# Attention: value products on every second query tile, the next head's hash products in front of them, exponentials placed by tile

## The chip, the cores and the metric

The kernel runs on one core of a Trainium2 chip. The metric is the device time of one execution in microseconds, the median of several runs. A core has engines with a queue each, which run side by side and wait for each other through semaphores: TensorE (PE in the profile, its weight loads PEld), VectorE (DVE), ScalarE (ACT), GpSimd (POOL), and SyncE (SP), whose queue here issues transfers alone.

## What is computed

Three stages, each fed by the one before. The change lies in the first.

```python
q_bits = (einsum('bhsd,dk->bhsk', q, proj) > 0)     # 6 hash bits
k_bits = (einsum('bhsd,dk->bhsk', k, proj) > 0)
mask = q_bucket[:, :, :, None] == k_bucket[:, :, None, :]
scores = where(mask, q @ k.T / sqrt(64), -1e9)
attn = softmax(scores);  x = attn @ v               # 2 x 8 heads, 768 x 64
x = moe(x)     # 1536 tokens of 512, top 1 of 8 experts, 512 -> 1024 -> 512
out = (x @ w_a) * (x @ w_b) @ w_out
```

## The kernel before

Attention goes through 16 heads (h) one after the other. A head has six query tiles (t) of 128 queries, and a tile is one step g = 6h + t of a single loop. The order of work on each engine is the order in which this loop writes it; nothing is moved afterwards. A step does the following.

- `scores(g + 1)` (L158, L159): four products on TensorE that put the next tile's 128 x 768 scores, hash bits included, into PSUM (`s`, two buffers).
- `smax(g + 1)` on VectorE: a minimum over the scores (L164, `mm`) and one small SCALAR_TENSOR_TENSOR (L165) that makes the scale and bias `sb` of the exponential.
- Work of other heads on TensorE, the "fill": the value products `av_step` of the head before (L200, `AV_AT` says which of its six key tiles go to which query tile), the output products `o_out` of two heads before (L238, tile 4), the hash products `hash_mm` of the next head (L128, `m`).
- `tposes(g, 0)` and `tposes(g, 1)` (L185, `tp`, two buffers of one half tile each): six transposes of the tile's exponentials `p`. Each half is copied from PSUM to `pt` ("eviction"), by ScalarE (L189) or VectorE (L191), as table `ev` says.
- `sexp(g + 1)` on ScalarE (L172, `p`): the next tile's exponentials. The table `se` gives for each t where it is written: 0 before the evictions of tile g, 1 between them, 2 behind them.
- Preparation of head h + 2: `split_a` on ScalarE (L103) writes `tq` at tile 2 and `tk` at tile 4 (`sa`: behind position 2 of tile 2, at position 1 of tile 4); `split_b` makes the rests, `bq` on VectorE and GpSimd (L115, L116) and `bk` on GpSimd alone (a TENSOR_TENSOR, L118, and a CAST, L119).
- At tile 1 `hash_codes` (L142) turns the hash products into bits, and four transfers on the SP queue (L147) put them into `tq` and `tk` of the next head. `load(h + 3)` is also written at tile 1, ahead of all else; its buffer is the one that the hash products of head h + 1 read last.
- At tile 5 `o_evac` on VectorE copies the finished value products out of PSUM (L220).

ScalarE, VectorE and GpSimd take their instructions strictly in the written order, which these lines of the step fix:

```python
side(0)          # sexp if se[t] == 0, hash_codes at tile 1
tposes(g, 0)
side(1)          # sexp if se[t] == 1, then split_a at tile 4
tposes(g, 1)
side(2)          # sexp if se[t] == 2, split_a at tile 2, split_b
```

The first head (h = 0) and the last (h = 15) have other fill; the expert layer (from about 268 us) and the last layer follow, and neither is touched.

Of the kernel before, what the change touches and what calls it, by code (L numbers as in the profile page):

```python
# [21 lines left out]
N, DM, E, FF, F2 = 1536, 512, 8, 1024, 1536  # L22
C = 224
GR = ((0, 6), (6, 4), (10, 2))
K = {'se': (0, 1, 2, 1, 1, 2), 'ev': (0, 0, 0, 1, 0, 1, 0, 0, 0, 1, 0, 0), 'avl': (), 'oul': 0, 'hml': 0, 'hc': ((0, 0), (0, 2), (1, 1), (2, 1)), 'sa': ((2, 2), (4, 1)), 'sb': ((3, 2), (4, 2)), 'ext': (1, 0, 2, 4, 7, 8), 'hm0': 0, 'hc0': ((1, 0), (1, 2), (3, 0), (4, 1))}
C_ID, C_TRI, C_THR, C_REV, C_TOK, C_IOTA, C_BASE, C_SLOT = 0, 128, 256, 258, 266, 278, 279, 287
CW = C_SLOT + C
FAR = 1024.0
AV_AT = {1: (0, 1), 2: (2,), 3: (3, 4), 5: (5,)}


@with_exitstack
def attn_moe_kernel(ctx: ExitStack, tc: tile.TileContext, xin, cst, projd, wblk, wmoe, w2in, out):
# [29 lines left out]
    pos = const.tile([128, 12], F32, name="pos")  # L63
# [29 lines left out]
    def load(h, first=()):  # L93
        X[h] = xp.tile([128, 2 * S], F32, tag="x", name="x")
        for i in range(2):
            after(nc.sync.dma_start(out=X[h][:, i * S:(i + 1) * S], in_=xin[h, :, i * S:(i + 1) * S]), first)
        V[h] = vp.tile([128, NT, D], F32, tag="v", name="v")
        nc.sync.dma_start(out=V[h], in_=xin[h, :, 2 * S:].rearrange("p (k d) -> p k d", d=D))
# [24 lines left out]
    def hash_mm(h, order=range(4)):  # L123
        p = (ps_m if h or 2 in order else ps_a).tile([128, 512], F32, tag="m" if h or 2 in order else "a", name="m")
        for j in order:
            i = j // 2
            hp_[h, j] = p
            PE.matmul(  # L128
                p[32 * j:32 * j + 32, :384], pst[:, 32 * i:32 * i + 32], X[h][:, j * 384:(j + 1) * 384],
                start=True, stop=True, skip_group_check=True,  # L130
            )
# [19 lines left out]
    def scores(g):  # L151
        h, t = divmod(g, NT)
        p = ps_s.tile([128, 2, 512], F32, tag="s", name="s")
        st[g] = p
        qs = slice(t * 128, t * 128 + 128)
        for c in range(2):
            sl = slice(c * 384, c * 384 + 384)
            PE.matmul(p[:, c, :384], T[h, 0][:76, qs], T[h, 1][:76, sl], start=True, stop=False)  # L158
            PE.matmul(p[:, c, :384], B[h, 0][:, qs], B[h, 1][:, sl], start=False, stop=True)  # L159

    def smax(g):
        m = mm[:, g % 4]
        sb = sm.tile([128, 2], F32, tag="sb", name="sb")
        DVE.tensor_reduce(out=m[:, 1:2], in_=st[g][:, :, :384], axis=AX.XY, op=ALU.min)  # L164
        DVE.scalar_tensor_tensor(  # L165
            out=sb, in0=m[:, 1:2].to_broadcast([128, 2]), scalar=BIG / 2, in1=m, op0=ALU.is_le, op1=ALU.mult
        )
        scl[g], nbs[g] = sb[:, 0:1], sb[:, 1:2]
# [9 lines left out]
    def tposes(g, half):  # L178
# [8 lines left out]
        src = ps[:, :384].rearrange("p (a b) -> p a b", a=3)  # L187
        if K["ev"][2 * t + half] == 0:
            ACT.activation(o, src, ACTF.Copy)  # L189
# [5 lines left out]
    def av_step(h, k):  # L195
        if k == 0:
            av[h] = ps_a.tile([128, 512], F32, tag="a", name="av")
        v = V[h][:, k]
        for c in range(2):
            PE.matmul(  # L200
                av[h][c * 64:(c + 1) * 64, :384], v, PT[h][:, k, c * 384:(c + 1) * 384],
                start=(k == 0), stop=(k == NT - 1), skip_group_check=True,
            )
# [261 lines left out]
    def w_load(n, part):  # L465
        if n < 64:
            RAW[n, part] = wraw.tile([128, 512], F32, tag=f"wr{part}", name=f"wr{part}")
            nc.sync.dma_start(out=RAW[n, part], in_=wmoe[n // 8, n % 8, :, part * 512:(part + 1) * 512])
# [126 lines left out]
    with tc.manual_schedule():  # L595
# [49 lines left out]
        def set_up(k):  # L645
            if k == 0:
                split_b(1, 0)
                POOL.tensor_copy(held, pt_[0][:, 0:1])
            elif k == 1:
                split_b(1, 1)  # L650
            elif k == 2:
                POOL.memset(oh, 0.0)
                zero = wraw.tile([128, 512], F32, tag="wr0", name="zero")
                POOL.memset(zero, 0.0)
                zeros.append(zero)
                DVE.tensor_copy(tri, cs[:, C_TRI:C_TRI + 128])
            elif k == 5:
                DVE.tensor_scalar(
                    out=tokc.bitcast(I32)[:, :, 0], in0=cs[:, C_TOK:C_TOK + 12], scalar1=-float(E * C), scalar2=None,
                    op0=ALU.add,  # L660
                )
                DVE.tensor_scalar(
                    out=base2, in0=cs[:, C_BASE:C_BASE + 8], scalar1=1.0 / 128, scalar2=None, op0=ALU.mult
                )
# [3 lines left out]
        L = NHD - 1  # L668
        acts = (x0_load, lambda: x_split(0), lambda: (w_split(0, 0, POOL), w_split(0, 1, POOL)), lambda: x_split(1), lambda: x_split(2),
                lambda: w_split(1, 0, POOL))  # L670
        extra = {}
        for at, f in zip(K["ext"], acts):
            extra.setdefault(divmod(at, NT), []).append(f)
        NG = NHD * NT
        qa, qb = (0, 4), (4, 2)
        for g in range(NG):
            h, t = divmod(g, NT)
            if t == 1 and h + 3 < NHD:
                load(h + 3)
            if g + 1 < NG:  # L680
                scores(g + 1)
                smax(g + 1)
            if g < NT:
                set_up(g)
            if 2 * NT <= g < 2 * NT + (E * C + N) // 256:
                for i in (g - 2 * NT,):
                    nc.sync.dma_start(
                        out=xr[i * 256:(i + 1) * 256].rearrange("(p r) d -> p r d", p=128),
                        in_=zeros[0].unsqueeze(1).to_broadcast([128, 2, 512]),
                    )  # L690
            if g == 6 * NT:
                for n in range(4):
                    for part in range(2):
                        w_load(n, part)
            if g == 10 * NT + 1:
                r = router(0)
                todo = [r["s1"], r["s1b"], None, lambda: (r["s2"](), r["s2c"]()), r["s2b"], r["s4"], r["s4b"]]
                for f in r["sc"]:
                    todo += [f, None]
                todo += [r["s4c"], r["s3"], r["s5"]]  # L700
            early, late = [], []
            if h < L:
                if h:
                    for k in AV_AT.get(t, ()):
                        early.append(lambda k=k: av_step(h - 1, k))
                if h > 1 and t == 4:
                    (late if K["oul"] else early).append(lambda: o_out(h - 2))
                if t == (0 if h else K["hm0"]):
                    (late if K["hml"] else early).append(lambda: hash_mm(h + 1))
            elif t < 3:  # L710
                av_step(h - 1, 2 * t)
                av_step(h - 1, 2 * t + 1)
                if t == 0:
                    o_out(h - 2)
                if t == 2:
                    o_evac(h - 1)
            elif t == 3:
                o_out(h - 1)
            else:
                k = 3 * (t - 4)  # L720
                av_group(h, qa, (k, k + 1, k + 2))
                if t == 5:
                    o_evac(h, qa)
            for f in early:
                f()
            if h and h < L and t == 5 and not K["avl"].count(5):
                o_evac(h - 1)
            if g > 10 * NT + 1 and todo:
                f = todo.pop(0)
                if f:  # L730
                    f()

            def side(pos):
                if g + 1 < NG and K["se"][t] == pos:
                    sexp(g + 1)
                for i in range(2):
                    if h + 2 < NHD and K["sa"][i] == (t, pos):
                        split_a(h + 2, i)
                    if h + 2 < NHD and K["sb"][i] == (t, pos):
                        split_b(h + 2, i)  # L740
                if h < L and (t, pos) == (1, 0):
                    hash_codes(h + 1)

            side(0)
            tposes(g, 0)
            side(1)
            tposes(g, 1)
            for f in late:
                f()
            if h and h < L and t == 5 and K["avl"].count(5):  # L750
                o_evac(h - 1)
            side(2)
            for f in extra.get((h - L + 1, t), ()):
                f()
# [578 lines left out]
```

## Time and profile before

| | |
|---|---|
| median of 3 runs | 750.09 us (749.51 to 750.5) |
| the profiled execution, its own time | 749.55 us |
| its span, first to last instruction | 747.7 us |
| TensorE busy | 728.7 us (97% of the span) |
| VectorE, ScalarE, GpSimd busy | 527.3, 434.4, 279.4 us |
| granted TensorE clock, mean | 0.997 |

The time of a run is about 1.9 us more than the span; what lies around the span is not in the trace. Busy time of TensorE is modelled from starts and sizes, so a busy TensorE may still be waiting a little. Rows of the timeline give the start of an instruction (or of several alike in a row, "x6") and its length; two starts tell how long a piece of work really took, the wait included. A wait in square brackets is idle time of the engine just before, and who ended it.

### The profile page before, as it was taken

How to read it: one execution, taken by the hardware profiler on the slowest of the kernel's cores; microseconds unless marked ns; L12 is line 12 of the kernel's file. 1: busy time of each engine (PE TensorE's matmuls, PEld its weight loads, DVE VectorE, ACT ScalarE, POOL GpSimd, SP SyncE). 2: the span in 40 equal slices, each digit the busy share in tenths (PEclk: the TensorE clock that was granted, in tenths of full speed). 3: DMA queues.
4: the chain of work that ended last, by engine and by line, in shares of the span. 5: the costliest groups of instructions: out<-in, count | busy, mean ns of one | idle time of the engine just before them, and what ended most of it. 6: DMA issues, size and time to landing. Idle time of an engine off the chain costs nothing.

```text
span 747.7 us, 13437 instructions
## 1 busy us (share of the span) xinstructions
PE 728.7 (97%) x4621; PEld 617.5 (83%) x4622; DVE 527.3 (71%) x1033; ACT 434.4 (58%) x945; POOL 279.4 (37%) x319
## 2 busy tenths in 40 slices
PE   8899999999999999999999999999999999999995
PEld 6666666666666699999999999999999988999984
DVE  6787777778787777778779876778676245756641
ACT  6777777777777546666677744444554334344331
POOL 3222232322434265122111123444434466565543
PEclk9999999999999999999999999999999999999998
DMA  7367251221302038788897754545463332212202
GB/s 237 116 225 262 77 172 58 71 98 61 114 33 61 15 110 287 225 192 235 267 339 227 221 159 151 219 162 215 165 214 116 111 101 69 85 47 81 58 1 88
DMA packets 49594, 107.37 MB, mean 144 GB/s; under 512 B 8096, under 2 KB 11504, under 8 KB 47984
## 3 DMA queue, kind: packets, MB, share of 16 engines
q1 hardware_dynamic: 46848, 99.94, 41.4%
q0 software_dynamic: 2304, 6.31, 2.3%
q8 instruction: 38, 0.62, 0.4%
q14 instruction: 36, 0.29, 0.1%
q10 hardware_dynamic: 368, 0.20, 0.1%
HBM read 82.76 MB, written 22.56 MB: 141 GB/s over the span
## 4 chain that ended last, share of the span: by engine, by line
PE 80%; DVE 8%; ACT 5%; issue 4%; POOL 1%; DMA 1%; SPq 0%; DVEq 0%; POOLq 0%; ACTq 0%
PE tp L185 8%; PE av L200 8%; PE y L934 5%; PE acc L1056 4%; PE acc L1055 4%; PE acc L1057 4%; PE h L896 3%; PE h L895 3%; PE h L894 3%; PE s L158 3%; PE s L159 3%; ACT p L172 3%; PE y L935 3%; DVE mm L164 2%; PE abb L894 2%
## 5 line engine op out<-in xcount | busy, mean ns | idle before, releaser
L164 DVE TENSOR_REDUCE mm<-s 128x1 f32<-128x768 f32 x96 | 91.8, 956 | 31.5 <-PE s L159 27.1
L185 PEld LDWEIGHTS tp<-cs,p 128*128 128x128 f32 x576 | 62.1, 140 | 55.3 <-ACT p L172 35.9
L853 POOL TENSOR_TENSOR pc<-t,pc 128x256 fp32r<-128x256 f32 x86 | 74.8, 893 | 84.1 <-ACT pc L852 84.1
L172 ACT ACTIVATE p<-s,sb 128x768 f32<-128x768 f32 x96 | 95.0, 989 | 15.9 <-PE tp L185 8.9
L189 ACT ACTIVATE pt<-tp 128x384 f32<-128x384 f32 x144 | 67.0, 489 | 45.5 <-PE tp L185 44.3
L185 PE MATMUL tp<-cs,p 128*128 128x128 f32 x576 | 83.4, 281 | 6.8 <-ACT p L172 5.1
L478 DVE TENSOR_TENSOR wl<-wr,wh 128x512 fp32r<-128x512 f32 x125 | 81.0, 688 | 8.3 <-ACT wh L477 3.5
L477 ACT ACTIVATE wh<-wr 128x512 fp32r<-128x512 f32 x128 | 73.7, 624 | 4.0 <-DMA wr<-wmoe 3.9
L934 PE MATMUL y<-hl,wh 128*128 128x448 f32 x224 | 74.9, 378 | 0.2
L158 PE MATMUL s<-tk,tq 76*128 76x384 f32 x192 | 73.1, 381 | 0.3 <-DVE tq L135 0.3
L894 PE MATMUL h<-xh,wh 128*128 128x224 f32 x256 | 71.4, 279 | 0.2 <-ACT xh L411 0.2
L200 PE MATMUL av<-pt,v 128*64 128x384 f32 x360 | 71.1, 503 | 0.0
L896 PE MATMUL h<-xh,wl 128*128 128x224 f32 x256 | 70.6, 276 | 0.2 <-DVE wl L478 0.2
L895 PE MATMUL h<-xl,wh 128*128 128x224 f32 x256 | 70.2, 274 | 0.3 <-DVE xl L412 0.3
L159 PE MATMUL s<-bk,bq 128*128 128x384 f32 x192 | 65.0, 339 | 0.0
L935 PE MATMUL y<-hl,wl 128*128 128x224 f32 x224 | 59.5, 266 | 0.0
L1055 PE MATMUL acc<-h,gh 128*128 128x512 f32 x144 | 56.7, 394 | 0.4 <-ACT gh L1041 0.4
L1056 PE MATMUL acc<-l,gh 128*128 128x512 f32 x144 | 56.8, 395 | 0.0
L1057 PE MATMUL acc<-h,gl 128*128 128x512 f32 x144 | 56.7, 394 | 0.0
L865 POOL TENSOR_TENSOR l<-t,h 128x512 fp32r<-128x512 f32 x24 | 31.0, 1292 | 64.7 <-ACT h L864 64.7
L116 POOL CAST bq<-tq 64x768 fp32r<-64x768 f32 x15 | 19.3, 1288 | 89.3 <-ACT tq L103 87.4
L907 ACT ACTIVATE hl<-h 128x224 fp32r<-128x224 f32 x64 | 22.8, 356 | 47.6 <-PE h L896 46.8
(225 smaller groups left out, 1889.9 us busy)
## 6 DMA issues: line engine op xcount, KB each, us to landing
wr<-wmoe SPq DMA_DIRECT2D x128, 256.0 KB
r<-w2in SPq DMA_DIRECT2D x12, 1536.0 KB
x<-xin SPq DMA_DIRECT2D x30, 384.0 KB
w<-t SPq DMA_DIRECT2D x36, 256.0 KB
t<-w SPq DMA_DIRECT2D x36, 256.0 KB
xr<-zero SPq DMA_DIRECT2D x13, 512.0 KB
xg<-xr SPq DMA_DIRECT2D x14, 256.0 KB
v<-xin SPq DMA_DIRECT2D x16, 192.0 KB
```

Source lines behind the costliest of these rows:

```text
L158: PE.matmul(p[:, c, :384], T[h, 0][:76, qs], T[h, 1][:76, sl], start=True, stop=False)
L159: PE.matmul(p[:, c, :384], B[h, 0][:, qs], B[h, 1][:, sl], start=False, stop=True)
L164: DVE.tensor_reduce(out=m[:, 1:2], in_=st[g][:, :, :384], axis=AX.XY, op=ALU.min)
L172: ACT.activation(p.rearrange("p (c n) -> p c n", c=2), st.pop(g)[:, :, :384], ACTF.Exp, scale=scl.pop(g), bias=nbs.pop(g), accum_out=sums[ ...
L185: PE.transpose(ps[:, j * 128:(j + 1) * 128], pt_[g][:, k * 128:(k + 1) * 128], ident)
L200: PE.matmul(av[h][c * 64:(c + 1) * 64, :384], v, PT[h][:, k, c * 384:(c + 1) * 384], start=(k == 0), stop=(k == NT - 1), skip_group_check= ...
L894: PE.matmul(ps, wh, xh, start=first, stop=False)
L895: PE.matmul(ps, wh, xl, start=False, stop=False)
L896: PE.matmul(ps, wl, xh, start=False, stop=last)
L934: PE.matmul(p, wh[:, w], hl, start=(f == 0), stop=False, skip_group_check=True)
L1055: PE.matmul(acc[i], h[:, w], wh, start=(f == 0), stop=False)
L1056: PE.matmul(acc[i], h[:, w], wl, start=False, stop=False)
```

## The change

Three things change for the heads 1 to 14, and the tables for the first and the last head stay.

- The value products go two key tiles at a time to the query tiles 1, 3 and 5 (before: two, one, two, one to tiles 1, 2, 3, 5).
- The hash products of the next head move from tile 0 to tile 1, in front of the value products. Head 0 keeps them at tile 0.
- The exponential's place is now 2, 0, 2, 0, 2, 0 for the tiles 0 to 5 (before 0, 1, 2, 1, 1, 2).

```diff
-K = {'se': (0, 1, 2, 1, 1, 2), 'ev': (0, 0, 0, 1, 0, 1, 0, 0, 0, 1, 0, 0), ...
+K = {'se': (2, 0, 2, 0, 2, 0), 'se0': (0, 1, 2, 1, 1, 2), 'ev': (0, 0, 0, 1, 0, 1, 0, 0, 0, 1, 0, 0), ...
...
-AV_AT = {1: (0, 1), 2: (2,), 3: (3, 4), 5: (5,)}
+AV_AT = {1: (0, 1), 3: (2, 3), 5: (4, 5)}
...
             if h < L:
+                if t == (1 if h else 0):
+                    early.append(lambda: hash_mm(h + 1))
                 if h:
                     for k in AV_AT.get(t, ()):
                         early.append(lambda k=k: av_step(h - 1, k))
                 if h > 1 and t == 4:
                     (late if K["oul"] else early).append(lambda: o_out(h - 2))
-                if t == (0 if h else K["hm0"]):
-                    (late if K["hml"] else early).append(lambda: hash_mm(h + 1))
...
-                if g + 1 < NG and K["se"][t] == pos:
+                if g + 1 < NG and K["se" if 0 < h < L else "se0"][t] == pos:
                     sexp(g + 1)
```

TensorE, tiles 0 to 2 of head 2. `s` are scores, `m` from `pst` the hash products, `av` value products, `tp` transposes. Before:

```order
L159 MATMUL s<-bk,bq 128x384
L128 MATMUL m<-x,pst 32x384 x4
L185 MATMUL tp<-cs,p 128x128 x6
...
L159 MATMUL s<-bk,bq 128x384
L200 MATMUL av<-pt,v 64x384 x4
L185 MATMUL tp<-cs,p 128x128 x6
...
L159 MATMUL s<-bk,bq 128x384
L200 MATMUL av<-pt,v 64x384 x2
L185 MATMUL tp<-cs,p 128x128 x6
```

Now:

```order
L159 MATMUL s<-bk,bq 128x384
L185 MATMUL tp<-cs,p 128x128 x6
...
L159 MATMUL s<-bk,bq 128x384
L128 MATMUL m<-x,pst 32x384 x4
L200 MATMUL av<-pt,v 64x384 x4
L185 MATMUL tp<-cs,p 128x128 x6
...
L159 MATMUL s<-bk,bq 128x384
L185 MATMUL tp<-cs,p 128x128 x6
```

The tiles 0 and 2 have no fill between scores and transposes any more; tile 1 has the hash products and the value products in one piece.

ScalarE, from tile 3's evictions of a middle head to tile 0's of the next head. `p` is an exponential, `pt` an eviction, `tk` the split. Before:

```order
L189 ACTIVATE pt<-tp 128x3x128
L172 ACTIVATE p,sums<-s,sb 128x768
L189 ACTIVATE pt<-tp 128x3x128 x2
L172 ACTIVATE p,sums<-s,sb 128x768
L103 ACTIVATE tk<-x 128x768
L189 ACTIVATE pt<-tp 128x3x128 x2
L172 ACTIVATE p,sums<-s,sb 128x768 x2
L189 ACTIVATE pt<-tp 128x3x128 x3
```

Now:

```order
L189 ACTIVATE pt<-tp 128x3x128 x3
L103 ACTIVATE tk<-x 128x768
L172 ACTIVATE p,sums<-s,sb 128x768 x2
L189 ACTIVATE pt<-tp 128x3x128 x4
```

At tile 4 `tk` now stands in front of the exponential of tile 5, and the exponential of the next head's tile 0 in front of both evictions of tile 5. (Of the three evictions in the first row two are tile 3's and one is tile 4's; of the four in the last, two are tile 5's and two the next head's tile 0's.) The orders of VectorE, GpSimd and SP are as before.

## Rows read from the trace of the kernel before

**Rows 1.** Stretch of heads 1 to 14: engines' busy time, granted clock (PEclk), transfers
```profile
core 0: us, PE busy (x) PEld busy (x) DVE busy (x) ACT busy (x) POOL busy (x), PEclk, DMA share, GB/s
...
24.97:238.97 214.00, 210.76 (x1375) 139.52 (x1375) 168.69 (x329) 160.51 (x326) 68.22 (x65) 1.00 0.34 115
```
**Rows 2.** Timeline of TensorE, head 4: start, length, line, tiles
```profile
72.11 0.42 PE L158 MATMUL s<-tk,tq 76*128 76x384 f32 x1
...
72.99 1.51 PE L200 MATMUL av<-pt,v 128*64 128x384 f32 x8
...
75.06 0.42 PE L158 MATMUL s<-tk,tq 76*128 76x384 f32 x1
...
77.37 0.42 PE L158 MATMUL s<-tk,tq 76*128 76x384 f32 x1
...
80.32 0.42 PE L158 MATMUL s<-tk,tq 76*128 76x384 f32 x1
...
81.12 0.97 PE L238 MATMUL m<-wb,o 128*128 128x160 f32 x6
81.93 0.82 PE L185 MATMUL tp<-cs,p 128*128 128x128 f32 x6
82.50 0.42 PE L158 MATMUL s<-tk,tq 76*128 76x384 f32 x1
...
84.82 0.42 PE L158 MATMUL s<-tk,tq 76*128 76x384 f32 x1
...
85.70 0.85 PE L128 MATMUL m<-x,pst 128*32 128x384 f32 x8
86.67 0.88 PE L185 MATMUL tp<-cs,p 128*128 128x128 f32 x6
87.30 0.42 PE L158 MATMUL s<-tk,tq 76*128 76x384 f32 x1
```
**Rows 3.** Timeline of ScalarE, from tile 4 of head 4
```profile
82.46 0.49 ACT L189 ACTIVATE pt<-tp 128x384 f32<-128x384 f32 x1 [0.33 <-PE tp L185]
82.84 0.99 ACT L172 ACTIVATE p<-s,sb 128x768 f32<-128x768 f32 x1
...
83.81 0.84 ACT L103 ACTIVATE tk<-x 128x768 fp32r<-128x768 f32 x1
...
85.53 0.99 ACT L172 ACTIVATE p<-s,sb 128x768 f32<-128x768 f32 x1
...
87.63 0.99 ACT L172 ACTIVATE p<-s,sb 128x768 f32<-128x768 f32 x1 [1.01 <-PE tp L185]
```
**Rows 4.** Timeline of TensorE at the program's start, hash products of head 0
```profile
7.17 0.84 PE L128 MATMUL m<-x,pst 128*32 128x384 f32 x4
7.94 1.29 PE L619 MATMUL warm<-ones 128*128 128x128 bf16 x20
```
**Rows 5.** Timeline of TensorE's weight loads, tile 4 of head 4
```profile
80.94 0.91 PEld L238 LDWEIGHTS m<-wb,o 128*128 128x128 f32 x6
```
**Rows 6.** Timeline of VectorE and GpSimd, tile 5 of head 4 and tile 0 of head 5
```profile
84.49 0.16 DVE L165 SCALAR_TENSOR_TENSOR sb<-mm 128x2 f32<-128x2 f32 x1
...
84.78 1.83 POOL L118 TENSOR_TENSOR bk<-x,tk 64x768 fp32r<-64x768 f32 x1 [1.62 <-issue]
...
86.67 0.82 POOL L119 CAST bk<-tk 64x768 fp32r<-64x768 f32 x1
86.80 0.71 DVE L165 SCALAR_TENSOR_TENSOR sb<-mm 128x2 f32<-128x2 f32 x1
```
**Rows 7.** The same two engines at the end of head 13
```profile
223.03 1.83 POOL L118 TENSOR_TENSOR bk<-x,tk 64x768 fp32r<-64x768 f32 x1 [2.88 <-issue]
...
223.25 1.64 DVE L347 SCALAR_TENSOR_TENSOR rt_s<-rt_ez,rt_s 128x6 f32<-128x6 f32 x1
```
**Rows 8.** Timeline of ScalarE and the weight loads, head 0: transposes wait for evictions
```profile
14.04 0.86 ACT L189 ACTIVATE pt<-tp 128x384 f32<-128x384 f32 x2
...
14.57 0.69 PEld L185 LDWEIGHTS tp<-cs,p 128*128 128x128 f32 x6 [0.17 <-ACT pt L189]
```
**Rows 9.** Timeline of the SP queue, head 4: the load and the first code transfers
```profile
71.47 0.80 SPq L96 DMA_DIRECT2D x<-xin  x2
...
75.07 1.61 SPq L147 DMA_DIRECT2D tq<-code  x2
```

More of the change, by code (lines that the diff above doesn't have):

```diff
@@ L24 @@
 GR = ((0, 6), (6, 4), (10, 2))
-K = {'se': (0, 1, 2, 1, 1, 2), 'ev': (0, 0, 0, 1, 0, 1, 0, 0, 0, 1, 0, 0), 'avl': (), 'oul': 0, 'hml': 0, 'hc': ((0, 0), (0, 2), (1, 1), (2, 1)), 'sa': ((2, 2), (4, 1)), 'sb': ((3, 2), (4, 2)), 'ext': (1, 0, 2, 4, 7, 8), 'hm0': 0, 'hc0': ((1, 0), (1, 2), (3, 0), (4, 1))}
+K = {'se': (2, 0, 2, 0, 2, 0), 'se0': (0, 1, 2, 1, 1, 2), 'ev': (0, 0, 0, 1, 0, 1, 0, 0, 0, 1, 0, 0), 'avl': (), 'oul': 0, 'hml': 0, 'hc': ((0, 0), (0, 2), (1, 1), (2, 1)), 'sa': ((2, 2), (4, 1)), 'sb': ((3, 2), (4, 2)), 'ext': (1, 0, 2, 4, 7, 8), 'hm0': 0, 'hc0': ((1, 0), (1, 2), (3, 0), (4, 1))}
 C_ID, C_TRI, C_THR, C_REV, C_TOK, C_IOTA, C_BASE, C_SLOT = 0, 128, 256, 258, 266, 278, 279, 287
```

## The prediction

> **What bounds the kernel now.** I read the busy times by stretch first, then TensorE's timeline of one head, then the other engines around the place where the order changes. From 24.97 to 238.97 us, fourteen heads, TensorE is busy for 210.76 of 214.00 us and no other engine for more than 169 [rows 1]: TensorE sets the time there, and a change is worth what it takes from or adds to TensorE's sequence, its waits included. The timeline shows that sequence as steps [rows 2], counted from one tile's first score product to the next tile's: tile 1 2.95 (72.11 to 75.06), tile 2 2.31, tile 3 2.95, tile 4 2.18, tile 5 2.32, tile 0 2.48; together 15.19 a head. Only tile 0 holds a wait: its hash products take from 85.70 to 86.67, 0.97, though the same products with work right behind them took 0.77 [rows 4]. The transposes behind them started 1.14 after the exponential's start (85.53 to 86.67) [rows 2, 3], so the exponential ended that tile's fill, at a cost of 0.20.
>
> **What TensorE's own sequence becomes.** The pieces are the old ones in another grouping. Scores in front of full-size weights take 0.80 (80.32 to 81.12), in front of value products 0.88 (72.11 to 72.99); transposes behind full-size work 0.57 (81.93 to 82.50), behind value or hash products 0.63 (86.67 to 87.30); the value products of two key tiles 75.06 - 0.63 - 72.99 = 1.44 [rows 2].
>
> - Tiles 0 and 2 lose their fill: 0.80 + 0.57 = 1.37 each. No row of a middle head shows scores directly in front of transposes; between 0.80 and 0.88 I take 0.80, since the output products, like the transposes, use the whole array.
> - Tile 1 gains the hash products: 2.95 + 0.77 = 3.72. Hash directly in front of value products is not in the trace; 0.77 is the row without a wait, 0.97 the row with one, and I take the first.
> - Tiles 3 and 5 have two key tiles each, 2.95; tile 4 stays at 2.18.
>
> Sum 1.37 + 3.72 + 1.37 + 2.95 + 2.18 + 2.95 = 14.54, so 0.65 less a head, for the heads 1 to 14: **-9.1 us**, if nothing waits. On the 0.80, row and rule differ. The weights of the output products begin to load at 80.94, 0.18 before those products [rows 2, 5], while scores over all 128 rows still run. The Trainium skill (TensorE: Matmul & The Clock Gate, Part 3, The mechanism) says that a weight load overlaps running products only where the row groups differ; by it nothing would be hidden here. With 0.88 in place of 0.80 the gain would shrink by 0.16 a head, about 2 us in all; that lies inside my range.
>
> **What then waits.** ScalarE's order decides, at tile 4. I follow one head with the clock of head 4, whose tile-4 transposes start at 81.93.
>
> 1. ScalarE evicts the first half at 82.46 and is free at 82.84 [rows 3]. Before, the exponential of tile 5 came next and `tk` at 83.81. Now `tk` comes first: 82.84 to 83.68 (0.84). The exponential starts there, and the transposes can follow 1.14 later, at 84.82.
> 2. TensorE needs them at 82.50 + 0.88 + 1.44 = 84.82: no wait worth counting, and no slack either.
> 3. GpSimd's TENSOR_TENSOR for `bk` started 0.13 after `tk` ended (84.65 to 84.78) and took 1.83 [rows 3, 6]. So now it runs from 83.81 to 85.64, where it began at 84.78.
> 4. VectorE's order is unchanged, so the small SCALAR_TENSOR_TENSOR for the next head's tile 0 comes at 84.49 as before [rows 6]. Then it was 0.29 ahead of `bk`; now it falls into it. What that costs, two rows show: such an instruction that met `bk` took 1.64 and ended with it (223.25 + 1.64 = 224.89, `bk` 223.03 + 1.83 = 224.86) [rows 7], and the `sb` that met the CAST at 86.67 took 0.71 instead of 0.16 [rows 6]. So `sb` ends at 85.66, not 84.65.
> 5. The exponential follows 0.12 later (86.80 + 0.71 = 87.51 to 87.63) [rows 3, 6]: 85.78. Both evictions of tile 5 now stand behind it on ScalarE; the next instruction starts 0.97 after an exponential (82.84 to 83.81): 86.75.
> 6. There are two half-tile buffers, so the next head's first transposes need that eviction; they started 0.53 after an eviction did (14.04 to 14.57) [rows 8]: 87.28. TensorE reaches them at 84.82 + 0.63 + 0.80 = 86.25. It waits 1.03, and a few hundredths for the second half: **1.05 a head**.
>
> I count 13 of these, one for each `bk` of the heads 1 to 13, at tile 0 of the heads 2 to 14. Two odd places I leave at nothing and to the range, a microsecond each: tile 0 of head 1, whose exponential the old table still places and no fill covers now, and the end of head 13, where the router's operations on VectorE [rows 7] shift the steps. +13.65 - 9.1 = **+4.55 us**.
>
> Edits that I cost at nothing: what stands behind the late `sb` on VectorE (the copy of `av`, two small operations, the next minimum) is first needed by tile 1 of the next head, more than 1.4 us of scores and transposes later. The load of `x` waits for the hash products; it was issued at 71.47, when they ended [rows 9], and will go about 2 us later, but its first reader is the split at tile 2 of the following head, some 15 us on. The code transfers (75.07) keep their place, since `hash_codes` stays at tile 1. The other places of the exponential leave slack: at tiles 1 and 3 it is covered by 1.44 of value products.
>
> The profiled execution has 749.55 us; 749.55 + 4.55 = 754.1. It lies 0.54 under the median of the runs shown, so a median of **754.6**. About 0.2% (1.5 us) is what a measurement of this kernel can tell from no change.
>
> **The rivals.**
>
> *`sb` isn't held: faster.* The place is step 4. If `bk` starts more than 0.7 us later than I say, after 84.49, `sb` is through first: the exponential starts at 84.77, the eviction at 85.74, the transposes at 86.27, and TensorE waits 0.02 instead of 1.05. Then the 9.1 come through but for a microsecond in head 1: 742. For it: before, `bk` did come after. Against it: it started 0.13 after `tk` in this head, and `tk` now precedes an exponential of 0.97.
>
> *Half and half: no change.* The wait needs only to be 0.65 instead of 1.05 to cancel the gain; or the wait holds and the pieces are still smaller than I think. Steps 4 to 6 add seven lengths from rows that agree to a few hundredths, so I see no source for 0.4. Time 750.
>
> *The pieces cost more: slower still.* Hash products at 0.97 add 0.2 a head (2.8 us), scores at 0.88 up to 2: 758 to 759.
>
> *The change doesn't do what it says* can't be held: the two orders show it on TensorE and ScalarE.
>
> **How the numbers follow.** Forecast, the dearer pieces included (752 to 759) 0.78; `sb` not held, 742, 0.12; no change, 750, 0.09; slower by a cause not named here 0.01. The forecast's own range: one wait 0.15 shorter on 13 heads takes off 2, the dearer pieces add up to 4.5. The range given, 749.5 to 759, takes in the case without change and leaves out the fast one. Faster by over 0.2% 0.12, within 0.09, slower 0.79.
>
> **What would show it.** In the new trace: tile 1's score-to-score step near 3.7 and tile 2's near 1.4; `tk` directly behind tile 4's first eviction; an `sb` of about 1.1 us at tile 5 of every head 1 to 12, ending with `bk`; at tile 0 a wait of TensorE's transposes of about 1 us, put down to ScalarE's eviction or exponential; a period of about 15.6 us a head. If those `sb` take 0.16 and the period is 14.5, the forecast is wrong at step 4; if `sb` is long and the period is still under 15.2, at step 5 or 6.

## The result, and the profile after

The changed kernel takes 755.57 us (median of 4 runs, 754.34 to 756.49), the kernel before in the same comparison 750.28: a ratio of 1.0071, 95% interval 1.0053 to 1.0089. It is slower, as forecast (754.6, range 749.5 to 759). The profiled execution has 756.17 us, 6.62 more than before.

The stretch that answers to [rows 1], cut at the same instructions:

```profile
core 0: us, PE busy (x) PEld busy (x) DVE busy (x) ACT busy (x) POOL busy (x), PEclk, DMA share, GB/s
25.31:245.64 220.33, 207.33 (x1375) 141.54 (x1375) 170.00 (x329) 162.64 (x327) 70.17 (x65) 1.00 0.33 112
```

The fourteen heads take 220.33 instead of 214.00 us: +6.33, nearly the whole difference. TensorE is busy for 3.4 us less (207.33 against 210.76) and stands idle for 13.0 instead of 3.2. The granted clock is 1.00 in both. Who ended that idle time, the tile view of the transposes tells for the same stretch (us, times):

```profile
its engine sat idle before it (us, times) until:
  ACT pt L189: 11.0, 14
  ACT p L172: 2.0, 2
```

All 13.0 us lie in front of transposes, 11.0 of them put down to ScalarE's evictions. In the same view of before the transposes had 1.5 in front of them in all, put down to exponentials. So the regrouping did make TensorE's work shorter, and a new wait took more than that back. One head shows how. The timeline of TensorE from tile 1 of head 4 to tile 0 of head 5, the stretch of [rows 2]:

```profile
73.56 0.42 PE L158 MATMUL s<-tk,tq 76*128 76x384 f32 x1
...
74.45 0.85 PE L128 MATMUL m<-x,pst 128*32 128x384 f32 x8
75.23 1.51 PE L200 MATMUL av<-pt,v 128*64 128x384 f32 x8
...
77.31 0.42 PE L158 MATMUL s<-tk,tq 76*128 76x384 f32 x1
...
78.10 0.82 PE L185 MATMUL tp<-cs,p 128*128 128x128 f32 x6
78.68 0.42 PE L158 MATMUL s<-tk,tq 76*128 76x384 f32 x1
...
81.63 0.42 PE L158 MATMUL s<-tk,tq 76*128 76x384 f32 x1
...
83.23 0.82 PE L185 MATMUL tp<-cs,p 128*128 128x128 f32 x6
83.81 0.42 PE L158 MATMUL s<-tk,tq 76*128 76x384 f32 x1
...
86.14 0.88 PE L185 MATMUL tp<-cs,p 128*128 128x128 f32 x6
86.77 0.42 PE L158 MATMUL s<-tk,tq 76*128 76x384 f32 x1
...
88.58 0.93 PE L185 MATMUL tp<-cs,p 128*128 128x128 f32 x6 [0.86 <-ACT pt L189]
89.26 0.42 PE L158 MATMUL s<-tk,tq 76*128 76x384 f32 x1
```

From score to score, forecast in brackets: tile 1 3.75 (3.72), tile 2 1.37 (1.37), tile 3 2.95 (2.95), tile 4 2.18 (2.18), tile 5 2.96 (2.95), tile 0 2.49 (1.37 and a wait of 1.05). A head takes 15.70 (15.59), before 15.19.

The other engines in the same place, which answer to [rows 3] and [rows 6]; first ScalarE's timeline, then GpSimd's and VectorE's:

```profile
83.76 0.49 ACT L189 ACTIVATE pt<-tp 128x384 f32<-128x384 f32 x1 [0.59 <-PE tp L185]
...
84.15 0.84 ACT L103 ACTIVATE tk<-x 128x768 fp32r<-128x768 f32 x1
...
87.06 0.99 ACT L172 ACTIVATE p<-s,sb 128x768 f32<-128x768 f32 x1 [1.10 <-PE tp L185]
88.04 0.86 ACT L189 ACTIVATE pt<-tp 128x384 f32<-128x384 f32 x2
```
```profile
85.12 1.81 POOL L118 TENSOR_TENSOR bk<-x,tk 64x768 fp32r<-64x768 f32 x1 [0.64 <-POOL lg L250]
...
85.80 1.15 DVE L165 SCALAR_TENSOR_TENSOR sb<-mm 128x2 f32<-128x2 f32 x1
```

`bk` starts 0.13 after `tk` ends (84.99) and ends at 86.93; `sb` begins inside it, takes 1.15 where it took 0.16, and ends at 86.95; the exponential follows at 87.06, the evictions at 88.04, the transposes at 88.58. The trace puts ScalarE's wait of 1.10 down to `tp`, whose modelled end (86.14 + 0.88 = 87.02) comes at about the same moment as `sb`'s; the kernel with halves, below, tells the two apart.

### The profile page after: what moved, and what is told of

Read it like the earlier page. It is cut to its first block, busy times and chain, and to the rows that moved or that the text cites. A ratio compares the mean times of both kernels' runs of the same rounds, so it can differ in the third digit from the quotient of the medians.

```text
span 754.3 us, 13409 instructions
## 1 busy us (share of the span) xinstructions
PE 725.7 (96%) x4621; PEld 619.7 (82%) x4622; DVE 528.4 (70%) x1033; ACT 435.9 (58%) x945; POOL 281.1 (37%) x319
## 4 chain that ended last, share of the span: by engine, by line
PE 82%; ACT 5%; DVE 5%; issue 3%; DMA 2%; POOL 2%; ACTq 0%; SPq 0%; DVEq 0%; POOLq 0%
PE tp L185 9%; PE av L200 8%; PE y L934 5%; PE acc L1056 4%; PE acc L1055 4%; PE acc L1057 4%; PE s L159 3%; PE s L158 3%; PE h L896 3%; PE h L895 3%; PE h L894 3%; ACT p L172 3%; PE y L935 3%; PE abb L894 2%; PE aba L895 2%
## 5 line engine op out<-in xcount | busy, mean ns | idle before, releaser
L189 ACT ACTIVATE pt<-tp 128x384 f32<-128x384 f32 x144 | 65.4, 488 | 32.6 <-PE tp L185 32.6
L200 PE MATMUL av<-pt,v 128*64 128x384 f32 x360 | 68.1, 499 | 0.0
L116 POOL CAST bq<-tq 64x768 fp32r<-64x768 f32 x15 | 21.2, 1414 | 112.9 <-ACT tq L103 98.4
L894 PEld LDWEIGHTS h<-xh,wh 128*128 128x128 f32 x256 | 48.9, 191 | 1.7 <-ACT wh L477 0.5
```

The costliest lines, as they stand in the source:

```text
L200: PE.matmul(av[h][c * 64:(c + 1) * 64, :384], v, PT[h][:, k, c * 384:(c + 1) * 384], start=(k == 0), stop=(k == NT - 1), skip_group_check= ...
L894: PE.matmul(ps, wh, xh, start=first, stop=False)
```

## The experiments

Two theories were tested first. Mine: the loss is `sb`, held by GpSimd's `bk` because `tk` moved forward, and then the exponential and the evictions behind it. The rival: the loss comes from the order on ScalarE, from TensorE's new pieces, or from missing fill, and `sb` is long without harm. Edits are to the changed kernel unless said otherwise; ratios are to the kernel before, with their 95% intervals.

### The two parts of the change, each alone

The fill alone, with the exponentials at their old places:

```diff
-                if g + 1 < NG and K["se" if 0 < h < L else "se0"][t] == pos:
+                if g + 1 < NG and K["se0"][t] == pos:
```

> The kernel before with the new fill alone: value products on tiles 1, 3, 5 and hash products in front of the first, but the exponentials at their old places. Theory: tiles 0 and 2 have nothing left between scores and transposes, and the exponential behind one or both evictions comes too late there: waits of about 1.0 at tile 0 and 0.7 at tile 2, a head about 16.3, 765 us. Rival (the grouping saves its 0.5 a head wherever the exponentials stand): 744 us.

Measured: 766.09 us (764.61 to 766.99), ratio 1.0215 (1.0189 to 1.0242). Tiles 0 and 2, which lost their fill, wait for exponentials, as TensorE's timeline shows:

```profile
91.16 0.87 PE L185 MATMUL tp<-cs,p 128*128 128x128 f32 x6 [0.90 <-ACT p L172]
...
96.99 0.87 PE L185 MATMUL tp<-cs,p 128*128 128x128 f32 x6 [0.52 <-ACT p L172]
```

The places alone, in the kernel before with its old fill:

```diff
-K = {'se': (0, 1, 2, 1, 1, 2), ...
+K = {'se': (2, 0, 2, 0, 2, 0), 'se0': (0, 1, 2, 1, 1, 2), ...
...
-                if g + 1 < NG and K["se"][t] == pos:
+                if g + 1 < NG and K["se" if 0 < h < L else "se0"][t] == pos:
```

> The kernel before with the new places of the exponentials alone, fill and hash products as before. Theory: tk in front of the exponential makes bk hold sb at tile 5 (1.1 us), and with value products of one key tile there the transposes of tile 5 also wait about 0.5 for their exponential: a head about 15.8, 758 us. Rival (the fill at tile 0 hides it all): 750 us.

Measured: 758.28 us (756.41 to 759.3), ratio 1.0121 (1.0096 to 1.0146). The new places bring the hold by themselves, as its timeline of GpSimd and VectorE shows:

```profile
100.16 1.80 POOL L118 TENSOR_TENSOR bk<-x,tk 64x768 fp32r<-64x768 f32 x1 [0.63 <-POOL lg L250]
...
100.84 1.14 DVE L165 SCALAR_TENSOR_TENSOR sb<-mm 128x2 f32<-128x2 f32 x1
```

But the hold isn't what costs most here. Score to score, tile 0 takes 2.62 (before 2.48), while tile 5 takes 2.83 (before 2.32): it has one key tile as fill, and its transposes wait for the exponential that now stands behind `tk`, as TensorE's timeline shows:

```profile
101.06 0.87 PE L185 MATMUL tp<-cs,p 128*128 128x128 f32 x6 [0.45 <-ACT p L172]
```

So each part alone loses more (+16 and +8) than both together (+5.3): the new grouping needs the new places, the new places need the new grouping's second key tile at tile 5, and they make the collision.

### The hash products back at tile 0

```diff
-                if t == (1 if h else 0):
+                if t == 0:
```

> The changed kernel with the hash products back at tile 0, all else as changed. Theory: sb is held just as long (1.15), but TensorE has 0.85 more to do at tile 0 before it reaches the transposes, so the wait falls from 0.9 to about 0.2 and a head to about 15.0: 746 us. Rival (each moved piece is worth a fixed amount, the hash in front of the value products saves about 0.3 a head): 758 us or more.

Measured: 748.37 us (747.24 to 749.02), ratio 0.9972 (0.9957 to 0.9986). The timelines of GpSimd, VectorE and TensorE at tile 5 of head 3 and the tile after it:

```profile
67.33 1.82 POOL L118 TENSOR_TENSOR bk<-x,tk 64x768 fp32r<-64x768 f32 x1 [0.64 <-POOL lg L250]
...
68.01 1.16 DVE L165 SCALAR_TENSOR_TENSOR sb<-mm 128x2 f32<-128x2 f32 x1
...
69.86 0.85 PE L128 MATMUL m<-x,pst 128*32 128x384 f32 x8
70.80 0.93 PE L185 MATMUL tp<-cs,p 128*128 128x128 f32 x6
```

`sb` is held as long as ever, but the row of the transposes shows no wait: the hash products stand where TensorE would be idle. They take 0.94 (69.86 to 70.80), 0.16 more than in front of value products (74.45 to 75.23 in the changed kernel), so about 0.2 of the wait is left, as expected. A held `sb` costs only as much as is left uncovered. This version gives up part of the regrouping (15.07 a head) and is still faster than the kernel before.

### Taking the collision away, in three ways

First, `tk` behind tile 4's second eviction, so that `bk` comes after `sb` again:

```diff
-'sa': ((2, 2), (4, 1))
+'sa': ((2, 2), (4, 2))
```

> The changed kernel with one thing undone: at tile 4 the split that makes tk stands behind the exponential of tile 5 again. Theory (sb of the next head's tile 0 is held by bk's TENSOR_TENSOR on GpSimd): tk ends 0.97 later, bk begins behind sb, sb takes 0.16 again, TensorE's wait at tile 0 falls from 0.9 to under 0.1 and a head from 15.70 to about 14.7: 743 us. Rival (the wait comes from the exponential that now stands in front of both evictions of tile 5, whatever sb does): that order stays, so 755 us.

Second, `bk`'s subtraction on VectorE at tile 5, with no instruction of `bk` on GpSimd but the CAST:

```diff
-'sb': ((3, 2), (4, 2))
+'sb': ((3, 2), (5, 2))
...
-            (POOL if h else DVE).tensor_tensor(out=b[64:], in0=x[64:], in1=t[64:], op=ALU.subtract)
+            (POOL if h == 1 else DVE).tensor_tensor(out=b[64:], in0=x[64:], in1=t[64:], op=ALU.subtract)
```

> The changed kernel with ScalarE's and TensorE's orders untouched: bk's subtraction of heads 2 to 15 goes from GpSimd to VectorE, at the end of tile 5; GpSimd keeps the CAST. Theory: nothing long runs on GpSimd when sb comes, sb takes at most about 0.3, the wait at tile 0 is under 0.2 and a head about 14.8: 744 us, although VectorE gets about 1 us a head more. Rival (order of ScalarE alone): 755 us or more.

Third, `bk` left where it is, on GpSimd, as two instructions of half the columns:

```diff
-            (POOL if h else DVE).tensor_tensor(out=b[64:], in0=x[64:], in1=t[64:], op=ALU.subtract)
+            for c in ((0, 384), (384, 384)) if h > 1 else ((0, n),):
+                s = slice(c[0], c[0] + c[1])
+                (POOL if h else DVE).tensor_tensor(out=b[64:, s], in0=x[64:, s], in1=t[64:, s], op=ALU.subtract)
```

> The changed kernel with bk's subtraction on GpSimd in two halves of 384 columns each. Theory: sb is held by the instruction that runs, not by the work; the first half ends about 0.93 after it began, sb gets in between the halves and takes about 0.3 instead of 1.15; the wait at tile 0 falls from 0.9 to about 0.1: 745 us. Rival (GpSimd keeps what it holds from one half to the next): sb still ends with the second half, 755 us.

| | us | range | ratio (interval) |
|---|---|---|---|
| `tk` behind | 747.5 | 744.71 to 748.34 | 0.995 (0.993 to 0.9969) |
| `bk` on VectorE | 745.98 | 745.21 to 748.28 | 0.9937 (0.9917 to 0.9956) |
| `bk` in halves | 746.9 | 746.03 to 750.79 | 0.9953 (0.9933 to 0.9973) |

All three turn +5 into -3 to -4.5, and fall 2 to 4.5 us short of what I expected. The timelines of GpSimd and VectorE around tile 5 of head 4, in this order of kernels, for the third with TensorE and ScalarE too:

```profile
85.64 0.16 DVE L165 SCALAR_TENSOR_TENSOR sb<-mm 128x2 f32<-128x2 f32 x1
...
85.93 1.82 POOL L118 TENSOR_TENSOR bk<-x,tk 64x768 fp32r<-64x768 f32 x1 [1.61 <-issue]
```
```profile
84.59 0.16 DVE L165 SCALAR_TENSOR_TENSOR sb<-mm 128x2 f32<-128x2 f32 x1
...
85.94 0.95 DVE L118 TENSOR_TENSOR bk<-x,tk 64x768 fp32r<-64x768 f32 x1
```
```profile
83.61 1.96 POOL L120 TENSOR_TENSOR bk<-x,tk 64x384 fp32r<-64x384 f32 x2 [0.64 <-POOL lg L252]
...
84.29 0.33 DVE L167 SCALAR_TENSOR_TENSOR sb<-mm 128x2 f32<-128x2 f32 x1
...
84.64 0.88 PE L187 MATMUL tp<-cs,p 128*128 128x128 f32 x6
...
84.75 0.99 ACT L174 ACTIVATE p<-s,sb 128x768 f32<-128x768 f32 x1 [0.29 <-PE av L202]
```

The third is the sharpest: the order on every engine is that of the changed kernel (the line numbers are two higher), GpSimd even works longer (1.96), and only the point at which `sb` can come in between has moved. `sb` takes 0.33, and tile 0 takes 1.68 from score to score instead of 2.49 (1.50 in the two kernels above), so most of its wait is gone. The exponential starts 0.13 after `sb` ends (84.62 to 84.75), 0.11 after tile 5's transposes began: it was `sb` that it waited for, not `tp`. So ScalarE's order, the missing fill and dearer pieces don't make the loss without the held `sb`; the order and the fill decide how much of the hold reaches TensorE, as the kernel with the hash products at tile 0 shows and the next one does too.

### The exponential between the evictions of tile 5

This tests the last link: that the evictions behind the late exponential hold the transposes, and not the exponential's data alone.

```diff
-K = {'se': (2, 0, 2, 0, 2, 0), ...
+K = {'se': (2, 0, 2, 0, 2, 1), ...
```

> The changed kernel, but at tile 5 the exponential of the next head's tile 0 stands between the two evictions instead of in front of both (heads 1 to 14). Theory (the wait at tile 0 has two ends: the exponential, late because `sb` is held, and the evictions that stand behind it): `sb` is held as before (1.15) and the exponential starts at the same moment, but the first eviction is through before it, so the first three transposes need the exponential alone, 1.14 after its start. In the changed kernel's head 4 they would start at 87.06 + 1.14 = 88.20 instead of 88.58, 0.38 sooner; the second eviction, behind the exponential, may hold the other three by some hundredths. 0.3 to 0.4 less a head on 13 heads: -4 to -5, so 751. Rival 1 (the place in front of the evictions costs nothing, the exponential alone sets the end): no difference, 755.5. Rival 2 (any sooner start of the exponential that frees `sb` is what counts, the eviction in front of it makes it later): 757 or more.

Measured: 752.8 us (751.67 to 755.31), ratio 1.0044 (1.0026 to 1.0061). That is 2.8 below the changed kernel's median, less than expected, and the two ratios' intervals overlap a little (the changed kernel's begins at 1.0053), so the reading rests on the trace. The timelines of VectorE, ScalarE and TensorE:

```profile
84.51 1.15 DVE L165 SCALAR_TENSOR_TENSOR sb<-mm 128x2 f32<-128x2 f32 x1
...
85.82 0.98 ACT L172 ACTIVATE p<-s,sb 128x768 f32<-128x768 f32 x1
...
86.95 0.93 PE L185 MATMUL tp<-cs,p 128*128 128x128 f32 x6 [0.52 <-ACT p L172]
```

`sb` is held as before, the transposes start 1.13 after the exponential instead of 1.52 (87.06 to 88.58), and the wait that the trace gives is 0.52 instead of 0.86 and now ended by the exponential. A head takes 15.35 instead of 15.70, the 0.35 that was expected; some of it is lost again at tile 0 of head 14, which takes 2.15 instead of 1.41. Both ends exist, and in the changed kernel the eviction was the later one.

### The best versions

Halves, `tk` behind and, since head 1's tile 0 also waited, the hash products of head 2 left at tile 0 of head 1:

```diff
-                if t == (1 if h else 0):
+                if t == (1 if h > 1 else 0):
```

> Towards a better version: the changed kernel with tk behind the exponential, bk's subtraction in two halves, and the hash products of head 2 at tile 0 of head 1 as head 0 has them. Theory: no sb over about 0.3 before head 10, no wait of 0.9 at head 1's tile 0; 745 us. Rival (what is left lies elsewhere): 747 us, like each part alone.

Measured: **743.26 us** (742.73 to 744.36), ratio 0.9918 (0.9895 to 0.9942), faster than both kernels and the lowest median; its interval overlaps those of the next two. The same edit of head 1 with `bk` on VectorE:

> The kernel with bk's subtraction on VectorE, and the hash products of head 2 at tile 0 of head 1. Theory: the wait of 0.9 at head 1's tile 0 goes: 745 us. Rival: the wait moves to tile 1 and nothing is gained, 746 us.

Measured: 744.82 us (743.84 to 746.75), ratio 0.994 (0.9918 to 0.9961). And with `tk` behind, but `bk` in one instruction:

> The changed kernel with `tk` behind tile 4's second eviction and the hash products of head 2 at tile 0 of head 1, but `bk` in one instruction. It parts the two edits that lay between 747.5 and 743.3. Theory (head 1's tile 0 waits 0.9 for want of fill; the halves add nothing in a steady head where `bk` comes late enough, but take away the odd holds of `sb`, two of which cost some 2 us together in the profiled run): 745 to 746.5, with head 1's tile 0 free of its wait. Rival 1 (the halves did all of it): 747.5. Rival 2 (head 1 did all of it): 743.3.

Measured: 745.02 us (744.68 to 747.21), ratio 0.9927 (0.99 to 0.9953). With `tk` behind and `bk` whole, one place is left open, in both kernels that have it. At head 2, `bk` and `sb` are released by the same minimum and start together; from the timelines of GpSimd, VectorE, ScalarE and TensorE of the last kernel:

```profile
52.78 1.81 POOL L118 TENSOR_TENSOR bk<-x,tk 64x768 fp32r<-64x768 f32 x1 [3.86 <-DVE mm L164]
...
52.79 1.82 DVE L165 SCALAR_TENSOR_TENSOR sb<-mm 128x2 f32<-128x2 f32 x1
...
54.73 0.99 ACT L172 ACTIVATE p<-s,sb 128x768 f32<-128x768 f32 x1 [2.03 <-DVE sb L165]
...
56.25 0.93 PE L185 MATMUL tp<-cs,p 128*128 128x128 f32 x6 [1.93 <-ACT pt L189]
```

0.01 late, and `sb` is held for all of `bk`. This execution took 747.21 us, the other three of its kernel 744.68 to 745.11: the difference is about this one wait. With `tk` behind alone, two of ten took 744.7 to 744.8 and the others 746.8 or more. That looks like a race that falls either way from one execution to the next; as only one execution of each kernel was profiled, it isn't shown, nor is it shown that the halves make the 1.8 us between 745.02 and 743.26. In the profiled execution with halves the two also started together, at 53.07, and `sb` took 0.16; whether the halves or the moment decided that, one profile doesn't tell. The best version's steps, from TensorE's timeline, and its stretch of fourteen heads:

```profile
68.75 0.42 PE L160 MATMUL s<-tk,tq 76*128 76x384 f32 x1
...
69.57 0.93 PE L187 MATMUL tp<-cs,p 128*128 128x128 f32 x6
70.25 0.42 PE L160 MATMUL s<-tk,tq 76*128 76x384 f32 x1
...
71.15 0.85 PE L130 MATMUL m<-x,pst 128*32 128x384 f32 x8
```
```profile
24.72:233.55 208.83, 206.39 (x1375) 141.50 (x1375) 161.43 (x332) 163.62 (x327) 71.67 (x79) 1.00 0.35 118
```

Hash to hash (71.15, and 85.86 a head on) is 14.71, and TensorE is idle for 2.4 us of the stretch.

## Why the prediction was right, step by step

Its case was the likeliest one, and the mechanism held at every step; one term of the sum and one count did not. Its clock and that of the trace after differ by 1.30 at tile 4's transposes (81.93 and 83.23); with that added to the forecast:

- **Steps 1 and 2.** `tk` at 84.14 forecast, 84.15 measured; tile 5's step 2.96 with no wait.
- **Steps 3 and 4.** `bk` at 85.11, measured 85.12; `sb`'s end at 86.96, measured 86.95. The three kernels without the collision show that this is the cause.
- **Step 5.** Exponential at 87.08 forecast, 87.06 measured; evictions at 88.05 and 88.04.
- **Step 6.** Transposes at 88.58, to the hundredth. Scores to transposes took 0.79 in tile 2, so TensorE would have reached them at 87.56, a wait of 1.02 (forecast 1.03). The trace writes 0.86, since it counts from modelled ends.

Scores in front of transposes take 0.79 (77.31 to 78.10), as the row of before had it, and not 0.88. So the sentence on weight loads that the prediction took from the Trainium skill (TensorE: Matmul & The Clock Gate, Part 3, The mechanism) was, taken alone, not borne out. Hash products in front of value products took 0.78 (74.45 to 75.23), where I took 0.77.

**What was mis-sized** is the sum of the pieces: 14.54 was forecast, and 14.71 is what a head takes where nothing holds `sb`. So the regrouping is worth 0.48 a head there, not 0.65, or 6.7 us instead of 9.1. The term that fell short is "Tiles 0 and 2 lose their fill: 0.80 + 0.57". For tile 2 it holds (1.37). Tile 0 takes 1.50 in the best version (68.75 to 70.25), 0.82 to the transposes and 0.68 from there, and the reason is that the link of step 6 still binds there a little. From the timelines of ScalarE and of TensorE's weight loads at tile 0 of head 4, then of the weight loads and TensorE at tile 0 of head 11:

```profile
69.03 0.86 ACT L191 ACTIVATE pt<-tp 128x384 f32<-128x384 f32 x2
...
69.57 0.69 PEld L187 LDWEIGHTS tp<-cs,p 128*128 128x128 f32 x6 [0.19 <-ACT pt L191]
```
```profile
173.75 0.69 PEld L187 LDWEIGHTS tp<-cs,p 128*128 128x128 f32 x6
173.85 0.82 PE L187 MATMUL tp<-cs,p 128*128 128x128 f32 x6
```

At head 4 the weight loads and the transposes both start 0.54 after the first eviction, and the second half 0.54 after the second one (69.41 to 69.95): both wait for their buffers. At head 11 TensorE comes later, since tile 5 before it took 3.18 instead of 2.96; there the loads begin 0.10 ahead of the transposes, and the tile takes 1.37 (173.06 to 174.43), as forecast. In the changed kernel, too, transposes to scores took 0.68 at tile 0, where 0.57 and "a few hundredths" were forecast; with 0.03 more at tile 1 that is most of the difference between a period of 15.70 and the forecast's 15.59.

The experiments' shortfall of 2 to 4.5 us has another source, since their steady heads take 14.71, 14.71 and 14.88, about what was expected (14.7 and 14.8 for the first two). It lies in single heads. Head 14, one of 13 counted, had no wait to lose (below); with `tk` behind, tile 0 of head 1 takes 3.77 (an `sb` of 1.29) where the changed kernel has 2.48, and that of head 3 takes 3.56 (an `sb` of 1.82); with `bk` on VectorE, tile 0 of the heads 12 and 13 takes 1.94 and 2.18 (an `sb` of 0.60 and of 0.83).

In the profiled execution the balance is +6.62 against +4.55. Counted from tile 0 to the next tile 0 and against the kernel before, ten heads (2 to 6, 8, 9, 11 to 13) lie 0.9 over their forecast together, and head 7, with one `sb` of 1.52 instead of 1.15, lies 0.5 over. Head 1 lies 0.9 over: its tile 0, left at nothing, waits 0.90. Head 10 lies 0.9 over, which was not foreseen: the router's operations stand on VectorE there, an `sb` of 0.77 (176.02) ends with a CAST of GpSimd at tile 4, and the transposes wait. TensorE's timeline at these two places:

```profile
26.28 0.87 PE L185 MATMUL tp<-cs,p 128*128 128x128 f32 x6 [0.90 <-ACT p L172]
...
178.43 0.93 PE L185 MATMUL tp<-cs,p 128*128 128x128 f32 x6 [0.57 <-ACT pt L189]
```

Against that, head 14 lies 1.3 under. The thirteenth wait, counted for its tile 0, did not come: there `bk` started 0.12 behind `sb` (228.81 and 228.93), and the tile takes 1.41 (230.45 to 231.86). So the wait was there 12 times and not 13, and that the odd places nearly cancel each other (+0.9, +0.9, -1.3) is luck.

Of the rivals, *`sb` isn't held* fell with the first row of `sb`. But its price, 742, is what the best version nearly reaches. *Half and half* fell with a wait of 1.02 instead of 0.65. *The pieces cost more* was wrong in both lengths that it named (0.78 for the hash products, 0.79 for the scores), though a head did come out 0.17 dearer by another way.

## What to carry to other kernels

When an instruction moves forward on an engine with slack, follow what it releases: here `tk` was 1 us earlier, so a GpSimd instruction was, and a VectorE instruction of 0.16 us that had slipped in 0.29 ahead of it came too late and set TensorE's period. Before moving a long GpSimd instruction off the place, try it in two halves: that keeps the order and costs GpSimd 0.15 us. And a fill that looks like dead weight between two dependent steps may cover a late engine; look at what it covers before regrouping it.

## What the runs showed of the hardware that was not expected

- How sharp the hold is: an `sb` that starts 0.01 after `bk` is held for 1.82, the whole of it, and one 0.29 ahead of it takes 0.16. The Trainium skill (SBUF — State Buffer, SBUF: two separate sides) says that a VectorE instruction with two SBUF inputs and a GpSimd instruction that reads SBUF want the same pair of ports, and that whichever starts first has it for the whole instruction. These rows agree, for an instruction of 128x2 too.
- That it ends with the GpSimd instruction and not with its engine's work: with two halves issued back to back `sb` took 0.33 and ended at 84.62, as the first half did (84.61), at a price of 0.15 (1.81 to 1.96) for GpSimd.
- What the lead of a weight load is worth. In the changed kernel six transposes took 0.58 to the next scores at tile 4 (83.23 to 83.81), where the first load began 0.13 ahead of them:

```profile
83.10 0.71 PEld L185 LDWEIGHTS tp<-cs,p 128*128 128x128 f32 x6
```

They took 0.63 at tile 5, where it began with them (86.14 to 86.77), and 0.68 at tile 0, where the second half waited for its buffer besides (88.58 to 89.26).
